# K transposed on VectorE instead of TensorE, scores against a block-diagonal q tile, and one row of w2 laid out on 64 partitions

## The chip, the core and the metric

The kernel is one program on one of the eight cores of a Trainium2 chip. The metric is the device time of one execution in microseconds, as the median of repeated runs; a lower one is better. A core has five engines, each with its own queue of instructions: TensorE (PE, matmuls, with its weight loads shown as PEld), VectorE (DVE), ScalarE (ACT), GpSimd (POOL) and SyncE (SP, which here only issues DMAs). Each engine works through its queue in order, and waits on semaphores for the others. The DMAs of all queues run on the core's 16 DMA engines.

## What is computed

One decode step of a transformer block, for a batch B of 2 with one new token each, D = 576, all in bf16. With xn the normalized x:

```
x + attention(xn) @ wo + relu(xn @ w1 + b1)^2 @ w2 + b2
attention: 32 query heads, 16 KV heads (2 queries share one), head size 128,
           the last 2048 positions of a cache of 8192
scores = q k^T / sqrt(128);  p = softmax(scores);  o = p v
```

Per batch entry and KV head, 2048 rows of K and of V are read once, 33.6 MB in all; wq, wo, w1 and w2 add 20.0 MB. So 53.6 MB have to come from memory for very little arithmetic.

## The kernel before

**Units.** The work on the cache is cut into 8 units (NU). A unit u is a group of TH = 4 KV heads of one batch entry: `tq, b = divmod(u, B)`. K of a unit is one tile of 128 partitions by 8192 bf16 (2 MB); a partition holds 64 consecutive positions of one head, and the four heads alternate over the partitions (partition 4c + h). V is laid out in the same way. K and V share one pool of 6 such buffers (`kvpool`, line 85), which go round in order of allocation, so each load waits until an earlier K or V has been used up.

**One unit's chain.** `transposes` (L258) turns K, taken as f32 pairs of bf16, by 128 by 128 transposes on PE against an identity, four to a PSUM tile of 1024 bf16; each tile is copied to SBUF by ACT (even groups, L270) or DVE (odd groups, L272). `scores` (L274) multiplies it by `qz`, a constant tile that holds the q of each unit among zeros: the stationary tile is 128 by 32, and four matmuls run side by side in four strips of 32 columns of the PE array. A first matmul with `far_h` writes -1e30 where query and key are of different heads. `softmax` (L288) takes the row maximum on DVE (L291), widens it (L293), takes the maximum over partitions with a GpSimd library call (`partition_all_reduce`, L295, tile `gmax`), forms the bias on DVE (L298), exponentiates on ACT (L302) and transposes p in 32 by 32 blocks on DVE (L305). `pv` (L314) multiplies by V, `pv_end` (L326) adds four partial results on DVE (L333, L335), and its `fin` (L338) sums over partitions on PE, divides, and writes the result to `ws` (L344 to L351).

**The order.** `step(u)` (L387) does the transposes and scores of unit u, `pv` of unit u-2 between them, and `softmax(u)`. All matmuls and transposes on PE keep the order of the source (the helpers `matmul` and `transpose`, L93 and L96, so nearly all PE work is shown at L94 and L97). The other engines' orders are chosen by the scheduler. After step 6, `mlp_h` (L356) computes the hidden layer from w1, which occupies the one `wbig` buffer; when its matmuls are done, `wo` is loaded into that buffer, followed on SP by w2 in pieces: `w2a` (rows of the first half), `w2b` (9 rows of each partition, in a K/V buffer) and `w2c` (6, 2 and 1 rows). Then come step 7, `pv_all(6)`, `pv_all(7)`, and `out_acc` (L216): four matmuls for each row of wo (32 rows) and w2 (36 rows), accumulated in `out_ps`; a copy by ACT and one DMA end the kernel.

**SP's queue**, in order: k0, wq, k1, v0, k2, v1, k3, v2, k4, v3, k5, v4, k6, v5, w1, k7, v6, v7, wo, w2a, w2b, w2c in three. In front of the loop, `q_block` (L226) computes q from wq, copies it with repetition to `qrow`, transposes it four times and copies it into `qz`.

Of the kernel before, what the change touches and what calls it, by code (L numbers as in the profile page):

```python
# [16 lines left out]
def kernel(  # L17
# [14 lines left out]
    nc = tc.nc  # L32
# [17 lines left out]
    JG = 8  # L50
    NG = NJ // JG
# [5 lines left out]
    TG = NG // NT  # L57
    QZ = 2 * NC
    assert SR == 32 and NG % NT == 0

# [15 lines left out]
    W2P = [(9, 15), (15, 17), (17, 18)]  # L76
    R9 = 9
# [15 lines left out]
    def matmul(*a, **k):  # L93
        tc.keep_in_program_order(nc.tensor.matmul(*a, **k))  # L94

# [20 lines left out]
    def issue_flat(w, name):  # L116
        n = w.shape[0] * w.shape[1] // P
        tl = wbig.tile([P, NH * L1], BF16, tag="wbig", name=name)
        nc.sync.dma_start(out=tl[:, 0:n], in_=w.rearrange("r n -> (r n)").rearrange("(p l) -> p l", p=P))
        return tl  # L120

    const.tile([P, 144], F32, name="pad_0")
# [15 lines left out]
    tmp_f = work.tile([P, 2, Dh], F32, tag="tmp", name="tmp_f")  # L138
# [50 lines left out]
    nc.vector.tensor_scalar(out=off[:], in0=own[:], scalar1=BIG, scalar2=-BIG, op0=ALU.mult, op1=ALU.add)  # L189
    of_h = const.tile([P, NC * WC], F32, name="of_h")  # L190
# [20 lines left out]
    w2c_sb = w2pool.tile([P, (FR - R9) * D], BF16, name="w2c")  # L211
# [8 lines left out]

    qz = const.tile([P, NQ, B, 2, 3 * QZ], BF16, name="qz")
    nc.gpsimd.memset(qz[:], 0.0)
# [3 lines left out]
    def q_block():  # L226
        for t in range(NH):
            for g in range(NG4):
                o = t * LQ + g * QW
                matmul(q_ps[32 * g:32 * g + 2 * B, :], lhsT=xnT[:, t].rearrange("p x b -> p (x b)"),  # L230
                       rhs=wq_sb[:, o:o + QW], start=(t == 0), stop=(t == NH - 1), skip_group_check=True,
                       tile_position=(0, 32 * g))
        row_t = const.tile([RB, 4 * HW], BF16, tag="row", name="qrow")
        qrow = row_t[:, 0:2 * QW]
        nh = QH // 2
        for k in range(2):
            cp = nc.scalar.copy if k else nc.vector.tensor_copy
            cp(out=qrow[:, k * QW:(k + 1) * QW].rearrange("p (i a d) -> p i a d", a=2, d=Dh),  # L238
               in_=q_ps[0:RB, k * QW // 2:(k + 1) * QW // 2].rearrange("p (i d) -> p i d", d=Dh).unsqueeze(2)
               .to_broadcast([RB, nh, 2, Dh]))  # L240
        qrow_f = qrow.bitcast(F32)
        qT_ps = psum.tile([P, QH * P], F32, tag="sc", bufs=2, name="qT_ps")
        for i in range(QH):
            transpose(out=qT_ps[:, i * P:i * P + RB], in_=qrow_f[:, i * Dh:(i + 1) * Dh],
                      identity=ident_f[0:RB, 0:RB])
        qT_v = qT_ps[:].bitcast(BF16).rearrange("p (i g e x b c) -> p b x g c e i", g=NG4 // 2, e=2, x=32 // B, b=B, c=2)
        hd = Dh // 2
        for j2 in range(2):
            cp = nc.scalar.copy if j2 else nc.vector.tensor_copy
            pp = slice(hd * j2, hd * (j2 + 1))  # L250
            o = QZ + NC * j2
            for b in range(B):
                for half in range(2):
                    cp(out=qz[pp, half * NQ // 2:(half + 1) * NQ // 2, b, :, o:o + NC].rearrange(  # L254
                        "p g c (e i) -> p g c e i", e=2), in_=qT_v[pp, b, half])

    kT_tiles, sc_tiles, pT_tiles, o1_tiles, o_tiles = {}, {}, {}, {}, {}
    def transposes(u, g):  # L258
        k_f = k_tiles[u][:].bitcast(F32)
        kT_ps = psum.tile([P, JG * P], BF16, tag="kT", bufs=3, name=f"kT_ps_{u}_{g}")  # L260
        kT_f = kT_ps[:].bitcast(F32)
        for i in range(JG // 2):
            j = g * JG // 2 + i
            transpose(out=kT_f[:, i * P:(i + 1) * P], in_=k_f[:, j * P:(j + 1) * P], identity=ident_f[:])
        t, o = divmod(g, TG)
        if o == 0:
            kT_tiles[(u, t)] = ktpool.tile([P, TG * JG * P], BF16, tag="kT_sb", name=f"kT_{u}_{t}")
        kT = kT_tiles[(u, t)][:, o * JG * P:(o + 1) * JG * P]
        if g % 2 == 0:
            nc.scalar.copy(out=kT, in_=kT_ps[:])  # L270
        else:
            nc.vector.tensor_copy(out=kT, in_=kT_ps[:])  # L272

    def scores(u, t):  # L274
        tq, b = divmod(u, B)
# [4 lines left out]
        kT = kT_tiles.pop((u, t))[:].rearrange("p (j k c) -> p j k c", k=P, c=2)  # L280
        z = QZ * (1 - t)
        for c in range(2):
            for g in range(4):
                matmul(sc_ps[32 * g:32 * (g + 1), :], lhsT=qz[:, tq, b, c, z:z + SR],
                       rhs=kT[:, :, 32 * g:32 * (g + 1), c], start=False, stop=(t == NT - 1 and c == 1),
                       skip_group_check=True, tile_position=(0, 32 * g))

    def softmax(u):  # L288
        sc_ps = sc_tiles.pop(u)
        m1 = work.tile([P, 1], F32, tag="m1", name=f"m1_{u}")  # L290
        nc.vector.tensor_reduce(out=m1[:], in_=sc_ps[:], axis=AX.X, op=ALU.max)  # L291
        m2 = work.tile([P, NC], F32, tag="m2", name=f"m2_{u}")
        nc.vector.tensor_scalar(out=m2[:], in0=off[:], scalar1=m1[:, 0:1], scalar2=None, op0=ALU.add)  # L293
        gmax = work.tile([P, NC], F32, tag="gmax", name=f"gmax_{u}")
        nc.gpsimd.partition_all_reduce(gmax[:], m2[:], channels=P, reduce_op=ReduceOp.max)  # L295
        gown = work.tile([P, NC], F32, tag="gown", name=f"gown_{u}")
        bias = work.tile([P, 1], F32, tag="bias", name=f"bias_{u}")
        nc.vector.scalar_tensor_tensor(out=gown[:], in0=gmax[:], scalar=-scale, in1=own[:], op0=ALU.mult,  # L298
                                       op1=ALU.mult, accum_out=bias[:])
        p_sb = work.tile([P, NJJ * 32], BF16, tag="p_sb", bufs=1, name=f"p_{u}")  # L300
        o1 = keep.tile([P, Dh + 1], F32, tag="o1", name=f"o1_{u}")
        nc.scalar.activation(out=p_sb[:], in_=sc_ps[:], func=ACT.Exp, bias=bias[:, 0:1], scale=scale,  # L302
                             accum_out=o1[:, Dh:Dh + 1])
        pT = keep.tile([P, NJJ, SR], BF16, tag="pT", name=f"pT_{u}")
        nc.vector.transpose(out=pT[:].rearrange("p j r -> p (j r)"), in_=p_sb[:])  # L305
        pT_tiles[u] = pT
        o1_tiles[u] = o1
# [4 lines left out]
    nc.gpsimd.memset(hT_sb[:], 0.0)  # L312

    def pv(u, part, parts):  # L314
        n = NJJ // parts
        if part == 0:
            o_tiles[u] = psum.tile([P, NS * Dh], F32, tag="o", name=f"o_ps_{u}")
        v = v_tiles[u][:].rearrange("p (t j s d) -> p j t s d", t=NT, s=2, d=Dh)
        for j in range(part * n, (part + 1) * n):
# [3 lines left out]
        if part == parts - 1:  # L323
            pT_tiles.pop(u)

    def pv_end(u):  # L326
# [3 lines left out]
        for k in range(NS):  # L330
            kw = dict(out=o1[:, 0:Dh], in0=o_ps[:, k * Dh:(k + 1) * Dh])
            if k == 0:
                nc.vector.tensor_scalar(scalar1=in_s[:, 0:1], scalar2=None, op0=ALU.mult, **kw)  # L333
            else:
                nc.vector.scalar_tensor_tensor(scalar=in_s[:, k:k + 1], in1=o1[:, 0:Dh], op0=ALU.mult, op1=ALU.add,  # L335
                                               **kw)

        def fin():  # L338
# [5 lines left out]
            nc.vector.reciprocal(out=linv[pp, :], in_=op[pp, Dh:Dh + 1])  # L344
            om_t = work.tile([P, Dh], F32, tag="om", name=f"om_{u}")
            om = om_t[pp, :].rearrange("p (q r) -> p q r", r=WR)
            nc.vector.scalar_tensor_tensor(out=om, in0=op[pp, 0:Dh].rearrange("p (q r) -> p q r", r=WR),
                                           scalar=linv[pp, 0:1], op0=ALU.mult, op1=ALU.mult,
                                           in1=own_c[pp, :].unsqueeze(2).to_broadcast([32, WC, WR]))
            with nc.allow_low_precision(reason="sums of one term and zeros"):  # L350
                nc.vector.tensor_reduce(out=ws[pp, :, BS * b], in_=om.rearrange("p q r -> p r q"), axis=AX.X,  # L351
                                        op=ALU.add)
# [3 lines left out]
    def mlp_h(w1_sb):  # L356
        h_ps = [psum.tile([P, HB], F32, tag="kT", bufs=3, name=f"h_ps_{k}") for k in range(2)]
# [28 lines left out]

    def step(u):  # L387
        fin = None
        w = u - 2
        with_pv = w >= 0  # L390
        for g in range(NG):
            transposes(u, g)
            if with_pv and g == 1:
                pv(w, 0, 2)
            if with_pv and g == 2:
                pv(w, 1, 2)
                fin = pv_end(w)
            if g == TG + 1:
                scores(u, 0)
            if g == TG + 2 and fin:  # L400
                fin()
        scores(u, 1)
        softmax(u)

    def pv_all(u):
        pv(u, 0, 1)
        pv_end(u)()

    for g in range(NG):
        transposes(0, g)  # L410
    q_block()
    for t in range(NT):
        scores(0, t)
    softmax(0)
    load_v(2)
    b1_rows = B_b1.rearrange("(x n) -> x n", n=HW)
    for i0, i1 in ((0, 2), (2, 4), (4, 6), (6, 8)):
# [3 lines left out]
    load_k(4)  # L421
# [16 lines left out]
    nc.sync.dma_start(out=w2a_sb[:], in_=w2_rows[0])  # L438
# [10 lines left out]
    for r in range(FR):  # L449
        w, o = (w2b_sb, r) if r < R9 else (w2c_sb, r - R9)  # L450
        out_acc(hT_sb[:, 1, r, :], w, o, stop=(r == FR - 1))
# [36 lines left out]
```

## Time and profile before

| | |
|---|---|
| median of 3 runs | 134.0 us (133.91 to 134.0) |
| the profiled execution | 133.92 us |
| its span, first to last instruction | 132.1 us |
| mean granted TensorE clock | 0.834 |
| busy: PE / PEld / DVE / ACT / POOL | 84.6 / 52.6 / 63.2 / 46.7 / 4.9 us |
| DMA moved, mean rate | 53.76 MB, 407 GB/s |
| DMA busy share of the SP queue's transfers | 95.2% of 16 engines' span |
| gmax of units 0 to 7 starts at | 28.29, 36.68, 45.63, 54.59, 63.78, 75.02, 83.97, 109.97 us |
| hidden layer's matmuls | 91.09 to 95.36 us |
| wo issued; first matmul with wo; last matmul | 95.41; 118.36; 129.24 us |

How to read it. The span is from the first to the last instruction of the one profiled execution, and all times within the kernel are counted from its start; the execution lasted 1.8 us longer than that. A busy time is the union of an engine's instructions, not what the kernel waits for. In a line of a group, "x8" is the number of instructions, then follow the busy time in us, the mean length of one in ns, and the idle time of the engine just ahead of them with what ended it. The chain that ended last is followed back from the end: each piece is what released the next.

### The profile page before, as it was taken

What the parts mean: (1) busy time and instruction counts of PE and PEld (TensorE: products, weight loads), DVE (VectorE), ACT (ScalarE), POOL (GpSimd) and SP (SyncE); (2) the same over time, 40 slices, a digit from 0 to 9 for tenths busy, and PEclk for the clock granted to TensorE, in tenths of its full rate; (3) what the DMA queues carried; (4) which work ended last, traced back from release to release, by engine and by line L of the source; (5) the groups of instructions that cost most, each with busy time, mean ns of one, the idle gap of its engine ahead of it and who ended that gap; (6) DMA issues with size and microseconds to landing.
All of it is one profiled execution on the core that took longest, in us unless ns stands there. A gap on an engine that the chain in (4) does not pass through costs nothing.

```text
span 132.1 us, 2285 instructions
## 1 busy us (share of the span) xinstructions
PE 84.6 (64%) x949; PEld 52.6 (40%) x949; DVE 63.2 (48%) x176; ACT 46.7 (35%) x67; POOL 4.9 (4%) x15
## 2 busy tenths in 40 slices
PE   0089319599589687697599787104819972739471
PEld 0069202286345353363455443002417640229360
DVE  7764400344557677396547687410075667550000
ACT  5725400339566085283256094200106632000000
POOL 5000000010010100100100100100000001000000
PEclk9999955959999999999779999855695999555955
DMA  4999899999999999999999999999999999899960
GB/s 160 397 437 526 369 388 442 422 432 432 429 432 422 442 417 427 437 432 437 432 427 414 437 488 402 445 424 405 427 427 442 468 435 458 376 408 418 418 255 1
DMA packets 3511, 53.76 MB, mean 407 GB/s; under 512 B 419, under 2 KB 558, under 8 KB 814
## 3 DMA queue, kind: packets, MB, share of 16 engines
q1 hardware_dynamic: 3456, 53.61, 95.2%
q8 instruction: 7, 0.11, 0.3%
q10 hardware_dynamic: 46, 0.02, 0.1%
q14 instruction: 2, 0.02, 0.0%
HBM read 53.62 MB, written 0.00 MB: 406 GB/s over the span
## 4 chain that ended last, share of the span: by engine, by line
DMA 78%; PE 15%; ACT 2%; SPq 1%; DVE 1%; issue 1%; ACTq 0%; DVEq 0%
DMA w<-in_B_w_dram 25%; DMA w2c<-in_B_w_dram 24%; DMA k<-in_A_k_cache_dram 16%; DMA wq<-in_A_wq_dram 13%; PE kT_ps L97 5%; PE h_ps L94 3%; PE q_ps L94 3%; PE sc_ps L94 2%; PE out_ps L94 1%; PE o_ps L94 1%; ACT kT L270 1%; DVE qrow L238 1%; SPq L106 0%; ACT qrow L238 0%; DVE qz L254 0%
## 5 line engine op out<-in xcount | busy, mean ns | idle before, releaser
L97 PE MATMUL kT_ps<-ident_f,k 128*128 128x128 f32 x256 | 41.4, 312 | 5.7 <-DMA k<-in_A_k_cache_dram 3.9
L97 PEld LDWEIGHTS kT_ps<-ident_f,k 128*128 128x128 f32 x256 | 32.9, 161 | 18.8 <-issue 9.9
L270 ACT COPY kT<-kT_ps 128x1024 bf16<-128x1024 bf16 x32 | 31.9, 1012 | 17.8 <-PE kT_ps L97 17.8
L272 DVE COPY kT<-kT_ps 128x1024 bf16<-128x1024 bf16 x32 | 21.8, 682 | 6.4 <-PE kT_ps L97 6.1
L94 PE MATMUL sc_ps<-kT,qz 128*32 128x512 bf16 x128 | 9.9, 388 | 6.7 <-DVE kT L272 4.7
L302 ACT ACTIVATE p<-sc_ps,bias 128x512 bf16<-128x512 f32 x8 | 5.5, 688 | 21.4 <-DVE gown L298 18.2
L94 PE MATMUL o_ps<-v,pT 128*32 128x512 bf16 x128 | 11.2, 429 | 0.0
L94 PEld LDWEIGHTS <-xnT 128*4 128x4 bf16 x108 | 3.5, 121 | 16.8 <-issue 15.2
L94 PE MATMUL h_ps<-w,xnT 128*4 128x288 bf16 x72 | 4.3, 429 | 8.0 <-DMA w<-in_B_w_dram 8.0
L305 DVE STREAM_TRANSPOSE pT<-p 128x512 bf16<-128x512 bf16 x8 | 5.7, 710 | 6.2 <-ACT p L302 6.2
L335 DVE SCALAR_TENSOR_TENSOR o<-o_ps,in_s,o 128x128 f32<-128x128 f32 x24 | 8.3, 345 | 0.4
L291 DVE TENSOR_REDUCE m<-sc_ps 128x1 f32<-128x512 f32 x8 | 5.5, 692 | 4.8 <-PE sc_ps L94 4.8
L375 DVE TENSOR_TENSOR hrow<-t 100x1152 bf16<-100x1152 f32 x2 | 2.6, 1355 | 9.6 <-ACT t L373 9.6
L94 PE MATMUL q_ps<-wq,xnT 128*4 128x512 bf16 x36 | 4.0, 627 | 4.9 <-DMA wq<-in_A_wq_dram 4.9
L295 POOL PARTITION_ALL_REDUCE gmax<-m x8 | 2.9, 367 | 104.9 <-DVE m L293 104.9
L94 PE MATMUL op_ps<-o,of_h 128*32 128x129 f32 x16 | 3.7, 316 | 4.6 <-DVE o L335 4.6
L456 ACT CAST fin_sb<-out_ps 113x144 bf16<-113x144 f32 x1 | 0.3, 280 | 17.9 <-PE out_ps L94 17.9
L94 PEld LDWEIGHTS <-qz 128*32 128x32 bf16 x128 | 2.1, 94 | 10.4 <-DVE kT L272 7.2
L97 PE MATMUL pro_ps<-ident,xn_sb 2*128 2x2 bf16 x5 | 0.9, 182 | 6.8 <-DVE xn_sb L171 6.5
L94 PEld LDWEIGHTS <-hT_sb 128*17 128x17 bf16 x144 | 3.4, 108 | 3.6 <-issue 3.5
L94 PE MATMUL out_ps<-wo,ws 128*17 128x144 bf16 x128 | 4.0, 325 | 1.2 <-DVE ws L351 1.2
L238 DVE CAST qrow<-q_ps 100x512 bf16<-100x512 f32 x1 | 0.7, 692 | 8.2 <-PE q_ps L94 8.2
(71 smaller groups left out, 57.4 us busy)
## 6 DMA issues: line engine op xcount, KB each, us to landing
k<-in_A_k_cache_dram SPq DMA_DIRECT2D x8, 2048.0 KB, 21.0
v<-in_A_v_cache_dram SPq DMA_DIRECT2D x8, 2048.0 KB, 21.5
w<-in_B_w_dram SPq DMA_DIRECT2D x1, 5184.0 KB
wq<-in_A_wq_dram SPq DMA_DIRECT2D x1, 4608.0 KB, 17.8
wo<-in_A_wo_dram SPq DMA_DIRECT2D x1, 4608.0 KB
w2a<-in_B_w_dram SPq DMA_DIRECT2D x1, 2592.0 KB, 26.9
w2b<-in_B_w_dram SPq DMA_DIRECT2D x1, 1296.0 KB
w2c<-in_B_w_dram SPq DMA_DIRECT2D x1, 864.0 KB
```

Source lines behind the costliest of these rows:

```text
L94: tc.keep_in_program_order(nc.tensor.matmul(*a, **k))
L97: tc.keep_in_program_order(nc.tensor.transpose(*a, **k))
L238: cp(out=qrow[:, k * QW:(k + 1) * QW].rearrange("p (i a d) -> p i a d", a=2, d=Dh), in_=q_ps[0:RB, k * QW // 2:(k + 1) * QW // 2].rearrang ...
L270: nc.scalar.copy(out=kT, in_=kT_ps[:])
L272: nc.vector.tensor_copy(out=kT, in_=kT_ps[:])
L291: nc.vector.tensor_reduce(out=m1[:], in_=sc_ps[:], axis=AX.X, op=ALU.max)
L295: nc.gpsimd.partition_all_reduce(gmax[:], m2[:], channels=P, reduce_op=ReduceOp.max)
L302: nc.scalar.activation(out=p_sb[:], in_=sc_ps[:], func=ACT.Exp, bias=bias[:, 0:1], scale=scale, accum_out=o1[:, Dh:Dh + 1])
L305: nc.vector.transpose(out=pT[:].rearrange("p j r -> p (j r)"), in_=p_sb[:])
L335: nc.vector.scalar_tensor_tensor(scalar=in_s[:, k:k + 1], in1=o1[:, 0:Dh], op0=ALU.mult, op1=ALU.add, **kw)
L375: nc.vector.tensor_tensor(out=h4[:, :, k * HB:(k + 1) * HB], in0=t4, in1=t4, op=ALU.mult)
L456: nc.scalar.copy(out=fin_sb[:], in_=out_ps[:])
```

## The change

K is transposed on DVE, two instructions for each unit, in blocks of 32 by 32 f32 pairs. The two copies out of PSUM and the PSUM tiles go. What this leaves in a column is spread over other partitions than with a full transpose, so `scores` now needs q placed block by block: the stationary tile is 128 by 128 and block-diagonal, and 16 matmuls of 512 columns use the whole array one after another. These tiles are made for each unit by a multiplication on GpSimd (`q_place`), alternately in two buffers, from the compact `qc`. DVE's instructions of a unit now keep the order of the source, and `step` has a new order. Row 17 of w2's second half goes to a tile `w2x` of 64 partitions with two rows each, by four DMAs behind w2a; `w2b` holds 11 rows and `w2c` 3, 2 and 1. b1 comes in 8 DMAs of one row instead of 4 of two; the load of k4 is issued before step 1.

```diff
-    qz = const.tile([P, NQ, B, 2, 3 * QZ], BF16, name="qz")
-    nc.gpsimd.memset(qz[:], 0.0)
+    qc = const.tile([P, NQ, B, NA, NC], BF16, name="qc")
+    qz = [const.tile([P, NA, P + QO], BF16, name=f"qz_{k}") for k in range(2)]
...
+    def q_place(u):
+        tq, b = divmod(u, B)
+        sh = [P, NA, NP4, NC]
+        nc.gpsimd.tensor_tensor(out=qz[u % 2][:, :, QO:].rearrange("p a (q c) -> p a q c", c=32)[:, :, :, 0:NC],
+                                in0=qc[:, tq, b].unsqueeze(2).to_broadcast(sh),
+                                in1=own_p[:].unsqueeze(1).unsqueeze(3).to_broadcast(sh), op=ALU.mult)
...
-    def transposes(u, g):
-        k_f = k_tiles[u][:].bitcast(F32)
-        kT_ps = psum.tile([P, JG * P], BF16, tag="kT", bufs=3, name=f"kT_ps_{u}_{g}")
-        for i in range(JG // 2):
...
-            transpose(out=kT_f[:, i * P:(i + 1) * P], in_=k_f[:, j * P:(j + 1) * P], identity=ident_f[:])
...
+    def transposes(u, t):
+        kT = ktpool.tile([P, UE // NT], BF16, tag="kT_sb", name=f"kT_{u}_{t}")
+        n = UE // NT // 2
+        tc.keep_in_program_order(nc.vector.transpose(out=kT[:].bitcast(F32),
+                                                     in_=k_tiles[u][:].bitcast(F32)[:, t * n:(t + 1) * n]))
+        kT_tiles[(u, t)] = kT
...
-        for c in range(2):
-            for g in range(4):
-                matmul(sc_ps[32 * g:32 * (g + 1), :], lhsT=qz[:, tq, b, c, z:z + SR],
-                       rhs=kT[:, :, 32 * g:32 * (g + 1), c], start=False, stop=(t == NT - 1 and c == 1),
-                       skip_group_check=True, tile_position=(0, 32 * g))
+        for i in range(NS // NT):
+            z = QO - NC * (t * NS // NT + i)
+            for h in range(2):
+                for e in range(2):
+                    matmul(sc_ps[:], lhsT=qz[u % 2][:, 2 * h + e, z:z + P], rhs=kT[:, i, :, h, :, e], start=False,
+                           stop=(t == NT - 1 and i == NS // NT - 1 and h == 1 and e == 1), skip_group_check=True)
...
     def step(u):
-        fin = None
         w = u - 2
-        with_pv = w >= 0
-        for g in range(NG):
-            transposes(u, g)
...
-        scores(u, 1)
-        softmax(u)
+        if w >= 0:
+            pv(w)
+        for t in range(NT):
+            scores(u, t)
+        fin = pv_end(w) if w >= 0 else None
+        rest = softmax(u)
+        if fin:
+            fin()
+        if u + 1 < NU:
+            q_place(u + 1)
+            transposes(u + 1, 0)
+        rest()
+        if u + 1 < NU:
+            transposes(u + 1, 1)
...
+    w2_last = w2_rows[1, :, RL * D:FR * D].rearrange("(e i q j) n -> e i j q n", e=2, i=2, q=4)
+    for i in range(2):
+        for e in range(2):
+            nc.sync.dma_start(out=w2x_sb[32 * i:32 * (i + 1), e, :], in_=w2_last[e, i])
```

`softmax` is cut in two: it issues the maxima and the all-reduce, and returns `rest`, which issues the bias, the exponential and the transpose of p. The hidden layer's values for `w2x` come from one more copy, transpose and two copies (`h_last`, `hx`, `hx_sb`).

In the built program, GpSimd's queue holds, ahead of each change between `q_place` and `gmax`, a pool configuration, the instruction pair that stands once in the program before. Its order is: configuration, q_place 0, 1 and 2, configuration, gmax 0, configuration, q_place 3, configuration, gmax 1, and so on to q_place 7, configuration, gmax 5, 6 and 7: 12 configurations for the one of before. q_place(u + 2) waits for the scores of unit u, whose tile it overwrites.

## The prediction, on record before the changed kernel was run

> **What bounds the kernel now.** I read the chain that ended last first, in order of time, then the groups by form, then GpSimd's own rows, then the timeline of a step.
>
> ```profile
> 33.63 20.86 DMA k<-in_A_k_cache_dram
> ...
> 58.00 33.05 DMA w<-in_B_w_dram
> 91.05 0.04 issue
> 91.09 4.30 PE h_ps L94 x71
> ...
> 96.74 31.12 DMA w2c<-in_B_w_dram
> 127.86 0.04 issue
> 127.90 1.36 PE out_ps L94 x36
> ```
>
> From 33.6 us on nearly all is a DMA in flight, and the queues' row on the page gives SP's transfers 95.2% of 16 engines' span. So the kernel streams 53.6 MB, and what the engines do is hidden as long as loads are issued in time. The steps before take 9.0 us (gmax starts at 36.68, 45.63, 54.59), against 9.75 us in which a unit's 4.2 MB arrive at 430 GB/s. Two places make compute count: wo can only be issued when the hidden layer's matmuls have ended (95.4; v7, ahead of it in the queue, runs out at 103.4, so there are 8 us to spare, less 1.4 us from an issue to its first packet), and the last work on units 6 and 7 must end before wo is due (wo's matmuls start at 118.4). A change that lengthens each of six steps by over 1 us uses this up.
>
> **The rows that price the change.**
>
> ```profile
> L272 DVE COPY kT<-kT_ps 128x1024 bf16<-128x1024 bf16 x32 | 21.8, 682 | 6.4 <-PE kT_ps L97 6.1
> L305 DVE STREAM_TRANSPOSE pT<-p 128x512 bf16<-128x512 bf16 x8 | 5.7, 710 | 6.2 <-ACT p L302 6.2
> L144 DVE STREAM_TRANSPOSE row<-tmp_f 128x32 f32<-128x32 f32 x1 | 0.2, 163 | 0.0
> ```
> ```profile
> L222 POOL MEMSET qz<- 128x768 bf16 x1 | 0.7, 739 | 0.3 <-POOLq L472 0.3
> ```
> ```profile
> L295 POOLq MODIFY_POOL_CONFIG  x2: 11/11/11, 2.5 to 2.6; - x2
> ```
> ```profile
> 28.29 0.37 POOL L295 PARTITION_ALL_REDUCE gmax<-m  x1 [25.79 <-DVE m L293]
> ```
>
> The reader is to see in them: (1) DVE transposes 512 bf16 in 710 ns and 32 f32 in 163 ns; (2) GpSimd writes 768 elements in 739 ns; (3) its pool configuration records 11 ns, but nothing used the configured library until 28.29.
>
> **Removed.** 256 transposes on PE (41.4 us busy), 32 copies on ACT (31.9) and 32 on DVE (21.8). All lie under the stream: worth nothing at the end by themselves.
>
> **K's transposes.** Two for each unit, 2048 f32 each. The two rows above give (710 - 163) / (512 - 32) = 1.14 ns per element and 0.13 us fixed: 2.46 us. Bounds: 1.4 us if they run at the copy's 0.67 ns per element, 4.8 us if a 4-byte element takes twice as long. I take 2.46, since one of the rows is f32 and shows no doubling. DVE's instructions keep the source order, so these stand in the chain of each step.
>
> **Scores.** 16 matmuls one after another instead of four strips side by side. In the trace, two that follow each other in one strip start 0.22 us apart (49.88 and 50.11, granted clock 1.0). At clock 0.5, q's 9 rounds of 512 columns took 4.04 us, 0.45 each. Eight of them wait for the second transpose: 1.9 us with the pipeline's tail, 3.7 at half clock. With long gaps on PE I take half clock (the rows of 84 to 95 us, when PE waited, have it).
>
> **q_place.** 512 elements on GpSimd. Bounds: 0.5 us at the memset's 0.96 ns, 1.5 with two reads beside the write. I take 1.0.
>
> **The pool configurations** decide. There were one, and are 12: six stand between q_place(u + 2), which itself waits until the scores of u are done, and gmax u. Queued behind each is gmax, for which DVE's bias waits, and behind that on DVE, in order, p's transpose, K's second transpose, and so the next scores. Below, the cost is nothing (11 ns); above, 25.7 us (2.56 to 28.29). A negative cost is excluded, as they are added in GpSimd's queue. Between: the packet records show wq's and K's packets at 38.5 to 39.6 ns per KB from 4 to 9 us, and 38.2 from 18 us on, as if something else read memory from 2.6 to about 9 us; ACT's table loads are over by 6. I take 6.4 us, though the slow packets may have another cause. Up to 3.0 us would be hidden: from the end of the scores, DVE needs 1.06 (maxima), 0.95 (`fin`) and 2.46 (first transpose of the next K), 4.5 in all, against 1.0 + 0.5 + configuration.
>
> The Trainium skill, "GPSIMD Engine Reference", section 2.1 Instruction dispatch, speaks against this change: the first call of a freshly loaded GpSimd kernel pays a load of its code of about 6 us, with no visible instruction. No row here shows that directly; by its 5.95 us instead of 6.4 the forecast would be 6 x 0.45 = 2.7 us lower.
>
> **The sum.** S_u is the end of unit u's scores, G_u that of its gmax. First unit: q_ps ends at 23.3; qrow's copies double in width (0.69 and 0.59 us for 512 columns: 1.2 and 1.0, one after the other), transposes and copies into qc 1.2, q_place 1.0, scores 5: S_0 = 32.9. G_0 = S_0 + 1.0 + 6.4 + 0.5 = 40.8. Then from G to the next G:
>
> ```profile
> 84.37 0.17 DVE L298 SCALAR_TENSOR_TENSOR gown<-gmax,own 128x8 f32<-128x8 f32 x1 [0.57 <-POOL gmax L295]
> 84.46 0.08 DVE L298 DVE_READ_ACCUMULATOR gown<-gmax,own 128x1 f32 x1
> 84.66 0.69 ACT L302 ACTIVATE p<-sc_ps,bias 128x512 bf16<-128x512 f32 x1 [3.15 <-DVE gown L298]
> 85.25 0.19 ACT L302 ACTIVATION_READ_ACCUMULATOR p<-sc_ps,bias 128x1 f32 x1
> 85.47 0.71 DVE L305 STREAM_TRANSPOSE pT<-p 128x512 bf16<-128x512 bf16 x1 [0.93 <-ACT p L302]
> ```
>
> This shows 1.84 us from gmax's end (84.34) to the end of p's transpose. Then K's second transpose 2.46, scores 3.7, q_place 1.0, configuration 6.4, gmax with its waits 0.5: **15.9 us a step**. (The configuration in front of q_place starts at G and ends 6.4 later, when the scores, at G + 8.0, are not done: hidden.) G_5 = 40.8 + 5 x 15.9 = 120.3, and S_6 = 128.3.
>
> From S_6 to the end PE leads: hidden layer 5.6 us (4.3 at the half clock of before, b1 and op); hrow's two products 3.0 as before, with p's and K's transposes between them on DVE 3.2; hidden transposes and copies 4.1 (98.4 to 102.5 before), for they hold the PSUM buffer that unit 7's scores need; these scores 4.5; from there to wo 9.6 before (108.8 to 118.4), plus 0.6 by the new order; 276 matmuls of out_acc 8.3 (before: 272 in 4.02 + 1.53 + 1.26 + 1.34); a wait of 1.1 like the 1.5 us at 123.8, which the profile calls issue and beside which lies an instruction packet of 16 KB. Sum 40.0: PE ends at 168.3 instead of 129.2, 39.1 later. wo, issued at about 134, has long landed. The end (0.3 copy, output) is as before. The profiled execution had 133.92: 133.92 + 39.1 = **173.0 us**; the median of the runs shown, 134.0, is 0.1 above it, which I leave out.
>
> **Edits hidden or small.** w2x: the records of the last row's packets (51 ns each, 8 on each DMA engine) end on eight engines at 126.7 to 127.3 us, on eight at 127.7 to 128.6, so one row less on the late ones is worth 0.4 us where the stream sets the end, and costs 0.4 if it goes to the late ones. The Trainium skill, "DMA: Bandwidth & Descriptors", section on why a DMA increments its semaphore by 16, says that a DMA uses as many engines as divide both outer sizes, here 8 of 32 and 8, the lowest; its rules for authors also say not to bother with partition halves. By the first rule this place is a gain of 0.4, by the second nothing; in my forecast the stream ends before PE and it is nothing either way. The two extra rounds of out_acc, hx's transpose and copies are 8 matmuls (0.3, counted) and four small copies beside other work. Eight DMAs for b1 instead of four, on ACT's queue, are done before ACT's first copy is due; four more issues of about 0.5 us on SP stand behind w2a, tens of us ahead of their data. k4's load moves ahead of step 1 past nothing but that step's issue-free work; its buffer comes free with K 1's second transpose (45 us), and SP waits there until then.
>
> **Rivals.**
>
> *A. The configurations cost under 3 us and DVE's chain is the bound.* Step: 1.06 + 0.95 + 2.46 + 1.15 (bias, exponential) + 0.75 + 2.46 + 1.9 = 10.7 us at full clock, 9.8 in the first two: S_6 = 95.4, PE ends some 39 later, at 134.4, 5.2 after 129.2: 139 us. For: nothing in the rows shows a configuration's cost. Against: the slow packets.
>
> *B. Faster.* If also a step takes at most 9.8 us (transposes of 2.0 us), S_6 comes by 90 and PE is done with wo's part in time; then the stream sets the end and w2x gives 0.4: 133.5 us. This decides at 9.8 us a step. For: 8 us to spare at wo, half the PE work gone. Against: the sum of rows is 0.9 above it.
>
> *C. f32 transposes at 4.8 us*, with the configurations: 2.35 more in each of six steps and in step 7: 173 + 16.5 = 190 us. Against: L144's 163 ns.
>
> That the change does not do what it says is excluded for PE and ACT: the built order has no K transpose there.
>
> **Chances.** Forecast 0.68, A 0.15, B 0.10, C 0.07. The forecast's own range: 4.5 us a configuration gives 161.6, 8.5 (then both of a step count) 188, full clock 11 less: 155 to 190. To leave out no more than 2 in 10 the range goes down to A: 136 to 190. A measurement of this kernel can tell about 0.2% (0.27 us) from no change. B's 0.10 is 0.07 faster, 0.02 the same, 0.01 slower; the rest is slower: 0.91.
>
> **What would show it.** Right: gmax starting 7 to 8 us after the scores end, 14 to 18 us apart in units 1 to 5, with DVE waiting for POOL; K's transposes at 2.4 to 2.5 us; DMA digits far under 9 after 55 us; wo issued near 134. Wrong: gmax within 2 us of q_place, steps of 10 to 11 us (A), or a chain that still ends in w2c's DMA (B).

## The result, and the profile after

The changed kernel takes **188.16 us** (median of 4 runs, 185.95 to 189.55) against 134.0 for the kernel before: a ratio of 1.391, with a 95% interval of 1.384 to 1.398. The profiled execution took 189.31 us (span 187.5, mean granted clock 0.727); two of the four runs, this one among them, lie over 1.5% above the fastest and are left out of the ratio.

The chain that ended last, which was one DMA after another before, now goes round through GpSimd. One step of it, from the maxima of unit 1 to the end of unit 2's scores (start, length, what):

```profile
52.66 0.70 DVE m L294
...
53.62 2.23 DVE kT L274
55.85 8.49 issue
64.33 0.40 POOL gmax L298
...
65.85 0.71 DVE pT L310
66.56 2.20 DVE kT L274
68.76 0.04 issue
68.80 3.58 PE sc_ps L96 x8
```

Of the 19.7 us from one end of the scores (52.64) to the next (72.38), 8.5 are "issue": GpSimd, whose next operation ends them, waits there for nothing that the profile shows. (PE works on the first half of unit 2's scores for 3.5 of these 8.5 us and loads run beside it, but the chain goes through neither.) Whom it holds up is told by the page's groups, whose last column is the idle time ahead of the group and what ended it:

```profile
L274 DVE STREAM_TRANSPOSE kT<-k 128x2048 f32<-128x2048 f32 x16 | 36.5, 2284 | 0.1
...
L303 DVE SCALAR_TENSOR_TENSOR gown<-gmax,own 128x8 f32<-128x8 f32 x8 | 1.3, 161 | 44.8 <-POOL gmax L298 44.8
...
L298 POOL PARTITION_ALL_REDUCE gmax<-m x8 | 3.1, 386 | 85.6 <-issue 57.1
...
L266 POOL TENSOR_TENSOR qz<-qc,own_p 128x128 bf16<-128x128 bf16 x8 | 3.1, 397 | 73.5 <-PE sc_ps L96 28.7
```

DVE waits 44.8 us for gmax, and GpSimd itself is idle for 57.1 us in front of six of its eight gmax with nothing to wait for, although it works for only 3.1 us on gmax and 3.1 on q. In that idle time lies only the pair of records of a pool configuration, and they are as short as in the kernel before (six pairs bear this line; the other six, in front of q_place, bear its line, with 4 to 108 ns):

```profile
L298 POOLq MODIFY_POOL_CONFIG  x12: 1/11/11, 34.2 to 132.0; - x12
```

So the price stands in no row of its own; it is read as the gap from the end of q_place to the start of gmax. The six gaps, as stretches of the timeline (length, POOL busy, granted clock, DMA share, GB/s):

```profile
core 0: us, POOL busy (x), PEclk, DMA share, GB/s
34.03:44.75 10.72, 0.01 (x2) 0.88 1.00 420
54.76:64.33 9.57, 0.00 (x1) 0.73 0.63 253
72.93:82.08 9.15, 0.00 (x1) 0.81 0.83 329
90.69:100.19 9.50, 0.01 (x2) 0.64 1.08 453
112.15:123.30 11.15, 0.00 (x1) 0.58 0.76 316
131.75:138.73 6.98, 0.01 (x1) 0.68 0.37 153
```

They are 9.5 us in the mean, and the shortest is the one in which the DMA engines did least. Otherwise their order is not that of the DMA share: the longest, 11.15 us, had 0.76. The loads have become the side work: their digits, nearly all 9 in the kernel before (first line), have holes in the changed kernel (second line) once the K and V buffers are held too long.

```profile
DMA  4999899999999999999999999999999999899960
```
```profile
DMA  6989999999599019913999989604700079899400
```

### The profile page after: what moved, and what is told of

It is laid out like the page before. It is cut to its first block, busy times and chain, and to the rows that moved or that the text cites. A ratio compares the mean times of both kernels' runs of the same rounds, so it can differ in the third digit from the quotient of the medians.

```text
span 187.5 us, 1780 instructions
## 1 busy us (share of the span) xinstructions
PE 85.5 (46%) x702; PEld 34.6 (18%) x702; DVE 80.0 (43%) x161; ACT 16.3 (9%) x38; POOL 8.8 (5%) x25
## 4 chain that ended last, share of the span: by engine, by line
DVE 29%; PE 28%; issue 25%; DMA 10%; ACT 4%; POOL 2%; SPq 0%; ACTq 0%; POOLq 0%
PE sc_ps L96 17%; DVE kT L274 15%; DMA wq<-in_A_wq_dram 10%; PE out_ps L96 4%; PE o_ps L96 3%; DVE pT L310 3%; ACT p L307 3%; DVE m L294 3%; PE q_ps L96 2%; DVE hrow L381 1%; POOL gmax L298 1%; DVE ws L357 1%; DVE o L341 1%; DVE om L353 1%; DVE m L296 1%
## 5 line engine op out<-in xcount | busy, mean ns | idle before, releaser
L96 PE MATMUL sc_ps<-kT,qz 128*128 128x512 bf16 x128 | 50.5, 567 | 64.8 <-DVE kT L274 64.5
L274 DVE STREAM_TRANSPOSE kT<-k 128x2048 f32<-128x2048 f32 x16 | 36.5, 2284 | 0.1
L96 PEld LDWEIGHTS <-qz 128*128 128x128 bf16 x128 | 16.3, 129 | 95.6 <-issue 92.2
L303 DVE SCALAR_TENSOR_TENSOR gown<-gmax,own 128x8 f32<-128x8 f32 x8 | 1.3, 161 | 44.8 <-POOL gmax L298 44.8
L96 PE MATMUL o_ps<-v,pT 128*32 128x512 bf16 x128 | 12.9, 481 | 0.0
L298 POOL PARTITION_ALL_REDUCE gmax<-m x8 | 3.1, 386 | 85.6 <-issue 57.1
L266 POOL TENSOR_TENSOR qz<-qc,own_p 128x128 bf16<-128x128 bf16 x8 | 3.1, 397 | 73.5 <-PE sc_ps L96 28.7
L96 PEld LDWEIGHTS <-xnT 128*4 128x4 bf16 x108 | 2.6, 95 | 15.1 <-issue 14.5
L96 PEld LDWEIGHTS <-pT 128*32 128x32 bf16 x128 | 4.6, 112 | 3.9 <-issue 2.4
L101 PE MATMUL hp<-ident,hrow 100*128 100x100 bf16 x18 | 1.7, 287 | 6.3 <-DVE hrow L381 6.3
L96 PEld LDWEIGHTS <-ws 128*17 128x17 bf16 x128 | 3.7, 136 | 1.5 <-DVE ws L357 1.5
L96 PE MATMUL sc_ps<-ident,far_h 4*128 4x512 bf16 x8 | 3.5, 439 | 0.0
```

The source lines that it names most:

```text
L101: tc.keep_in_program_order(nc.tensor.transpose(*a, **k))
L266: nc.gpsimd.tensor_tensor(out=qz[u % 2][:, :, QO:].rearrange("p a (q c) -> p a q c", c=32)[:, :, :, 0:NC], in0=qc[:, tq, b].unsqueeze(2).t ...
L274: tc.keep_in_program_order(nc.vector.transpose(out=kT[:].bitcast(F32), in_=k_tiles[u][:].bitcast(F32)[:, t * n:(t + 1) * n]))
```

## The experiments

My theory after this: the two kinds of GpSimd work, the multiplication of q_place and the all-reduce, exclude each other, each change between them costs some 10 us under the stream, and this alone is the loss. Rivals: the wait has another cause; the DVE chain and the full-array scores carry much of it.

**1. The change of kind by itself.** `mult` is a `tensor_tensor` of 128x128, `reduce` a `partition_all_reduce` of 128x8, both on GpSimd; during the second loop K and V are loaded.

```diff
+    for i in range(4):
+        mult()
+        reduce()
...
+    for i in range(5):
+        reduce()
+        mult()
```

> This kernel leaves out the whole block and writes zeros: GpSimd alternates between a multiplication of two 128x128 tiles and the all-reduce of a 128x8 tile, first with no load under way (9 changes, then three of each in a row), then while all of K and V stream (about 10 changes), then after the stream. Theory: each change of kind costs a library load that no record shows and that shares memory with the stream: 6 to 7 us from the end of one to the start of the next with no load (changed kernel, at 37% DMA share: 6.98), 9.5 to 11 us under the stream (at 100% share: 10.7), and nothing between two of a kind. Rival: what stood ahead of gmax was a wait on another engine, and the change of kind is cheap: under 1 us in all three stages. Second rival: a fixed price: the same 9 to 10 us in all stages.

Measured (stretches between two operations, columns as above; the first two lines lead to an all-reduce and to a multiplication with no load under way, the next four to a multiplication, an all-reduce, and again, under the stream, the last to a multiplication behind it):

```profile
18.90:24.80 5.90, 0.02 (x1) 1.00 0.00 0
25.20:31.80 6.60, 0.00 (x0) 1.00 0.00 0
...
83.40:95.10 11.70, 0.00 (x0) 1.00 1.00 422
95.60:106.40 10.80, 0.00 (x0) 1.00 1.00 422
106.90:118.90 12.00, 0.00 (x0) 1.00 1.02 426
119.40:129.20 9.80, 0.00 (x0) 1.00 1.01 426
...
151.30:158.10 6.80, 0.00 (x0) 1.00 0.00 0
```

With no load a change costs 5.9 to 6.1 us towards the all-reduce and 6.7 to 7.0 (once 7.7) towards the multiplication; with the DMA engines full, 9.9 to 10.9 and 11.6 to 12.2. Three of a kind in a row start without a gap (three all-reduces in 1.32 us). The first two changes, which were meant to be quiet, fell beside K's first loads and took 6.4 us (mean DMA share 0.75) and 10.2 us (0.47); so between no load and full engines the mean share of a gap does not give its length. Both rivals fall: the price is there with nothing to wait for, and it isn't fixed. The upper end under the stream is above the 11 us that I had given.

**2. The changed kernel without the changes of kind.** Two ways: q placed by ScalarE, and by GpSimd itself, but with copies (`nc.gpsimd.tensor_copy` in the same lines).

```diff
     def q_place(u):
-        nc.gpsimd.tensor_tensor(out=qz[u % 2][:, :, QO:].rearrange("p a (q c) -> p a q c", c=32)[:, :, :, 0:NC],
-                                in0=qc[:, tq, b].unsqueeze(2).to_broadcast(sh),
-                                in1=own_p[:].unsqueeze(1).unsqueeze(3).to_broadcast(sh), op=ALU.mult)
+        for q in range(NP4):
+            pp = slice(32 * q, 32 * (q + 1))
+            nc.scalar.copy(out=qz[u % 2][pp, :, QO + 32 * q:QO + 32 * q + NC], in_=qc[pp, tq, b])
```

> The changed kernel, but q goes to its diagonal places by four ScalarE copies of 32 partitions for each unit; GpSimd is left with the all-reduce and one configuration, all else as in the changed kernel. Theory (configurations hold the whole of each step up): the step falls from 18.8 us to m 0.95 + fin 0.95 + K's first transpose 2.27 + bias 0.2 + exponential 0.8 + p's transpose 0.71 + K's second 2.2 + half the scores 1.8 to 3.5 and gaps 0.1 = 10.0 to 11.7 us; scores of unit 6 end at 33.5 + 6 x 10.9 = 99 instead of 146.8, and with the same 37.9 us to the last matmul and 4.6 after it the time is 141 us (136 to 146). Rival (the DVE chain and the full-array scores at a low clock make up most of the 54 us): over 160 us.

> The changed kernel, with q placed by GpSimd itself and at the same places in its queue, but by four copies of 32 partitions instead of one multiplication; for copies the built program holds no configuration (one in all, as before). Theory (the change of library is the cost, not GpSimd's work in front of gmax): about 1 us of copies stands in front of gmax, beside the first transpose of the next K (2.27 us) and the rest of fin (0.95), so it is hidden: 136.4 us as with the copies on ScalarE (136 to 138). Rival (any GpSimd operation between scores and gmax costs the wait): over 180 us.

Measured: **136.43 us** with ScalarE (136.02 to 136.74; ratio to before 1.017, 1.015 to 1.019) and **137.06 us** with GpSimd's copies (136.36 to 137.34; 1.022, 1.020 to 1.024). 51 of the 54 us are gone. In GpSimd's timeline of the second, the copies start when the scores end, and gmax 0.20 us after the copies, held up only by the maxima:

```profile
43.34 0.94 POOL L267 COPY qz<-qc 32x32 bf16<-32x32 bf16 x4 [9.09 <-PE sc_ps L96]
44.48 0.37 POOL L297 PARTITION_ALL_REDUCE gmax<-m  x1 [0.20 <-DVE m L295]
```

So it is not work on GpSimd in front of gmax that costs the time, but the change of kind; the copies bring no configuration, and the built program holds one here as before. In this run it is recorded right in front of the first gmax, which starts 0.1 us behind it, with the DMA engines full:

```profile
L297 POOLq MODIFY_POOL_CONFIG  x2: 1/1/1, 33.8 to 33.8; - x2
```
```profile
33.90 0.36 POOL L297 PARTITION_ALL_REDUCE gmax<-m  x1
```

So a configuration as such costs nothing; what has the price is a change between the two kinds. (Experiment 1 has the same: its first multiplication, at 1.08 us, follows its configuration at 0.97.) Both kernels also end with that kind of operation, so its code may still have been in place from an execution before; no run tests that.

What remains of a step is DVE's chain with the second half of the scores, in the run with ScalarE:

```profile
71.00 1.91 PE sc_ps L96 x8
72.94 0.70 DVE m L293
...
74.90 2.31 DVE kT L273
77.39 0.79 ACT p L306 x2
78.20 0.71 DVE pT L309
78.91 2.21 DVE kT L273
81.16 1.91 PE sc_ps L96 x8
```

10.2 us here, 9.95 in the mean of six steps (scores of unit 0 end at 33.5, of unit 6 at 93.2): just over the 9.75 us of the stream. I had expected 141 us, since I put the end of unit 6's scores at 99, with steps of 10.9 us, the middle of 10.0 to 11.7 (half the scores at 1.8 to 3.5 us); in five of six steps half the scores took 1.9 us.

**3. The changes of kind alone, in the kernel before.**

```diff
         nc.gpsimd.partition_all_reduce(gmax[:], m2[:], channels=P, reduce_op=ReduceOp.max)
+        if u < 6:
+            dummy = work.tile([P, NC], F32, tag="dummy", name=f"dummy_{u}")
+            nc.gpsimd.tensor_tensor(out=dummy[:], in0=gmax[:], in1=gmax[:], op=ALU.mult)
```

> The kernel before, with one more GpSimd multiplication of 128x8 behind the all-reduce of units 0 to 5, whose output nobody reads: 13 configurations, and nothing else of the change. Theory: GpSimd needs two changes of kind of about 9.7 us for each unit, 20.2 us with the two operations, so gmax 6 starts at 28.3 + 6 x 20.2 = 149 instead of 84, and with the 41 us that the changed kernel needs from there the time is about 190 us (180 to 195). Rival (a configuration is cheap, the DVE chain costs the time): 134 to 136 us.

Measured: 184.84 us (182.03 to 188.63). Six multiplications of 0.2 us, whose output nobody uses, take the kernel before to nearly where the whole change took it:

```profile
28.51 0.37 POOL L295 PARTITION_ALL_REDUCE gmax<-m  x1 [26.01 <-DVE m L293]
39.87 0.20 POOL L298 TENSOR_TENSOR dummy<-gmax 128x8 f32<-128x8 f32 x1 [10.99 <-issue]
49.76 0.39 POOL L295 PARTITION_ALL_REDUCE gmax<-m  x1 [9.69 <-issue]
62.28 0.20 POOL L298 TENSOR_TENSOR dummy<-gmax 128x8 f32<-128x8 f32 x1 [12.13 <-issue]
```

Experiments 1 to 3 settle the cause: taken away, the loss goes; added alone, it comes; by itself, it has the size.

**4. Can the 2.4 us that remain be hidden?** DVE needs 8.85 us for a step, so I moved the next unit's first transpose and first half of scores ahead of the maxima.

```diff
     def step(u):
...
+        scores(u, 1)
         if u + 1 < NU:
             q_place(u + 1)
             transposes(u + 1, 0)
-        rest()
+            scores(u + 1, 0)
+        bias_exp, turn = softmax(u)
```

> The changed kernel with q placed by ScalarE, and a new order: the next unit's first K transpose and first half of scores stand ahead of the maxima, p v lies one unit deeper, and the hidden layer's transposes come after unit 7's scores. Theory: a step needs DVE for 2 x 2.27 + 0.95 + 1.5 + 0.2 + 0.95 + 0.71 = 8.85 us, under the 9.75 us in which a unit's data arrive, so the stream sets the end again: the last packets of w2c end at 128.4 us (copies on ScalarE: 128.43; before: 128.56), 133.8 us (133.4 to 134.2). Rival (the full-array scores at a granted clock near 0.5, 3.5 us a half, bind PE): a step of 10 us and 136 us.

Measured: 138.80 us (138.6 to 140.38; 1.038, 1.035 to 1.042): slower, against both expectations. From the maxima of one unit to those of the next it took 9.4, 7.6, 8.7, 10.2 and 10.3 us; in the last two half the scores took 3.5 and 3.4 us instead of 1.9, and DVE waited 1.4 and 1.3 us for them, as the rival had it. But at the end the order turned against itself (DVE's timeline, in brackets the idle time ahead and what ended it):

```profile
84.52 2.27 DVE L273 STREAM_TRANSPOSE kT<-k 128x2048 f32<-128x2048 f32 x1
96.77 2.31 DVE L273 STREAM_TRANSPOSE kT<-k 128x2048 f32<-128x2048 f32 x1 [9.98 <-DMA k<-in_A_k_cache_dram]
```

Unit 7's K comes behind w1, so its transpose waits 10 us, and the maxima of unit 6 and, on PE, the hidden layer stand behind it; wo was issued at 107.0 instead of 95.4. Mended by leaving unit 7 out of the look-ahead (`ahead` holds q_place, the first transpose and the first half of the scores), with w2x and with w2 as before:

```diff
+        if u + 1 < NU - 1:
+            ahead(u + 1)
...
+    pv_end(NU - 3)()
+    hrow = mlp_row(h_ps)
+    pv(NU - 2)
+    q_place(NU - 1)
+    transposes(NU - 1, 0)
```

> The last order mended where it lost: unit 7's K arrives behind w1 (its first transpose waited from 86.8 to 96.8 us there, and the maxima of unit 6, p v and the hidden layer's matmuls stood behind it), so unit 7's transposes and scores are no longer ahead of unit 6's; they follow the hidden layer's, p v of units 5 and 6 is drawn ahead of them. Theory: the steps at 8 to 10 us of the last run end unit 6's scores near 89 us, wo is issued by 98 us (in time is 102), unit 7 is done by 115, ahead of wo's landing at 118, and the stream sets the end: 134.2 us with w2x (133.9 to 134.6). Rival (what is left of the 2.4 us lies in the last unit's chain on DVE, whatever the order): 136 us or more.

> The same without w2x: w2's rows as in the kernel before (w2b 9 rows, w2c 6, 2 and 1), with K's buffers at a multiple of 512 bytes. Theory (w2x costs 0.4 us, as the aligned run of w2x alone measured, and the DVE transposes are hidden): 133.9 us (133.7 to 134.2), 0.2 to 0.5 below the run with w2x. Rival (w2x gains where the stream sets the end): 0.3 above it.

Measured: 135.07 us (134.37 to 135.75; 1.007, 1.005 to 1.010) and 135.32 us (134.11 to 135.98; 1.008, 1.005 to 1.011), both above what was expected, and the first below its rival's 136. The chain ends in DMAs again, in the run with w2x:

```profile
97.95 0.15 SPq L123
98.16 0.42 SPq L465
98.63 24.41 DMA w2x<-in_B_w_dram
123.06 6.79 DMA w2c<-in_B_w_dram
129.89 0.27 PE out_ps L96 x4
```

So DVE's transposes can be hidden but for about 1 us; no version beats the kernel before. What the last microsecond is remains open: w2c's last packet ends at 129.5 us here and at 129.0 in the run with the old w2, against 128.56 before, and single runs scatter over 1.9 us, more than the effect of w2x that the second run was to tell.

**5. w2x alone, and an address.**

```diff
-    W2P = [(9, 15), (15, 17), (17, 18)]
-    R9 = 9
+    R9 = 11
+    RL = FR - 1
+    W2P = [(R9, 14), (14, 16), (16, RL)]
...
+    for i in range(2):
+        for e in range(2):
+            nc.sync.dma_start(out=w2x_sb[32 * i:32 * (i + 1), e, :], in_=w2_last[e, i])
```

> The kernel before with only the last row of w2's second half on 64 partitions, two rows each, by four DMAs, and with w2b of 11 rows and w2c of 3, 2 and 1. Theory: the DMA engines that end late carry one packet of 51 ns for 8 partitions less: 133.6 us against 134.0 (133.4 to 133.8). Rival: the four small DMAs in front of w2b cost as much as they save, or the last packets go to the late engines: 134.0 to 134.4.

Measured: 135.34 us (135.0 to 135.57; 1.009, 1.008 to 1.011): 0.9% slower, and worse than the rival. In the packets' records nearly all were slower (those of 1,152 bytes alone kept 51 ns): 614 ns for 16,384 bytes instead of 611, from 20 us on, long before w2x. My edit had moved the K and V buffers to another start address. Three kernels part the two causes by a pad: w2x alone with 288 bytes more, the kernel before with 224 and with 256:

```diff
+    const.tile([P, 72], F32, name="pad_1")
...
+    const.tile([P, 56], F32, name="pad_1")
...
+    const.tile([P, 64], F32, name="pad_1")
```

> The run of w2x alone, with 288 bytes of padding, so that the K and V buffers start on a multiple of 512 bytes in a partition (31744) as in the kernel before (31232) and in the changed one (32768); without the padding they started at 31456. Theory: what w2x alone lost came from the address, since its K packets took 614 ns instead of 611 and its w2b packets 481 instead of 474 with copies on ScalarE; with the padding 133.8 us (133.5 to 134.1). Rival (the four small DMAs ahead of w2b, which put w2b's issue off by 5.2 us, cost it): 135.3 us again.

> The kernel before, with 224 bytes of unused padding behind the constants, so that all K, V and weight buffers start 224 bytes further on in a partition (31456 instead of 31232, no multiple of 512); nothing else is changed. Theory (the address slows the stream by about 0.5%): 135 us (134.7 to 135.4), K packets at 614 ns instead of 611. Rival (addresses don't matter): 134.0 us.

> The kernel before with 256 bytes of unused padding behind the constants: its buffers start at 31488, a multiple of 256 bytes and of 64, not of 512. Theory (only multiples of 512 run at the full rate): 134.85 us as with 224 bytes (134.6 to 135.1). Rival (multiples of 64 are enough): 134.0 us.

Measured: w2x on aligned buffers 134.39 us (134.24 to 135.32; 1.0035, 1.0019 to 1.0051); the kernel before with 224 bytes 134.85 us (134.72 to 135.1; 1.0067, 1.0055 to 1.0079), with 256 bytes 134.08 us (133.88 to 134.21; 0.9999, 0.9991 to 1.0008). The address is worth 0.8 us; a multiple of 256 is enough, and my "only multiples of 512" falls. w2x itself costs 0.37 us, where 0.2 gained was expected. Last, its four DMAs behind w2b instead of in front:

```diff
+    nc.sync.dma_start(out=w2b_sb[:], in_=w2_rows[1, :, 0:R9 * D])
     w2_last = w2_rows[1, :, RL * D:FR * D].rearrange("(e i q j) n -> e i j q n", e=2, i=2, q=4)
     for i in range(2):
         for e in range(2):
             nc.sync.dma_start(out=w2x_sb[32 * i:32 * (i + 1), e, :], in_=w2_last[e, i])
-    nc.sync.dma_start(out=w2b_sb[:], in_=w2_rows[1, :, 0:R9 * D])
```

> The aligned run of w2x alone, with its four DMAs issued behind w2b instead of in front of it, so that w2b is issued as early as in the kernel before. Theory (there is nothing to gain in w2x: 128 packets of 51 ns go and 128 come, and the packets of 1152 bytes add 9 ns a partition): 134.3 us again (134.2 to 134.5). Rival (w2b's later issue cost the 0.4 us, and the late engines do carry less): 133.6 to 133.9 us.

Measured: 134.43 us (134.27 to 135.51; 1.0032, 1.0010 to 1.0054). The place in SP's queue is not it.

## Why the prediction was right, and where it fell short

The mechanism, its place and the sign were right: six pool configurations between scores and gmax, with DVE, and by it PE and the loads, behind them. 173.0 us was 15 us too little, and the term that was mis-sized is the configuration.

- **The configuration behind q_place**, priced at 6.4 us: 10.7 in the first unit, 9.3 in the mean of the five steps. "As if something else read memory from 2.6 to about 9 us" gave a length, but those packets are no measure of a change of kind: in the run with GpSimd's copies, whose one configuration comes at 33.8 us, the packets from 4 to 6 us are as slow (41.8 and 40.5 ns per KB, and 37.9 to 38.5 from 6 to 9). Experiment 1 shows that 6.4 is within the price without load (5.9 to 7.0), to which the estimate came by luck, and that a full stream nearly doubles it. The same holds of the 6 us of the Trainium skill, "GPSIMD Engine Reference", section 2.1 Instruction dispatch: right where nothing else moves (5.9 to 6.1 us measured towards the all-reduce, 6.7 to 7.0 towards the multiplication), not under the stream (9.9 to 12.2); by it the forecast would have been 2.7 us further off.
- **The configuration in front of q_place**, costed at nothing because the scores cover it for 8.0 us: at 9 to 11 us the cover was too short twice. q_place of unit 3 started 1.73 us after the scores that release it (54.37 against 52.64), that of unit 6 3.52 us (111.76 against 108.24): 1.05 us a step. The forecast had named this case ("8.5, then both of a step count, 188") as the upper end of its own range. The kind of case came, but in two of five steps and with other terms smaller; that 188 is also the measured time is chance. So gmax came 7.5 to 15.1 us after the end of the scores, not 7 to 8, and 15.4 to 23.1 us apart, not 14 to 18.
- **The rest of the step.** q_place 0.40 instead of 1.0; K's transposes 2.28 (2.21 exposed) instead of 2.46, so no doubling for f32, and rival C falls; half the scores 3.4 to 3.6 instead of 3.7; gmax to the end of p's transpose 1.77 instead of 1.84. Per step: +2.9 and +1.05 for the two configurations, -0.6, -0.25, -0.2 and -0.1 for these: +2.8, and the end of gmax moved on by 18.8 us a step (45.14 to 139.13 in five) instead of 15.9.
- **The sum.** S_0 33.5 (32.9, though the terms as written add up to 32.7), G_0 45.1 (40.8), G_5 139.1 (120.3), S_6 146.8 (128.3), PE's end 184.7 (168.3). From S_6 on 37.9 us instead of 40.0: scores of unit 7 and what follows to wo took 17.0 instead of 14.7, but the hidden layer up to those scores 14.3 instead of 15.9 and out_acc 6.7 instead of 9.4, without the stall. wo was issued at 150.3, not near 134, and was never waited for, as foreseen.
- **Rivals A and B.** Experiment 2 is their condition, configurations at no cost: 136.4 us, between A's 139 and B's 133.5, with steps of 9.95 us between A's 10.7 and B's 9.8.
- **w2x** at 0.4 us gained where the stream sets the end: wrong in sign, 0.37 lost on aligned buffers. The step that failed is that one row less on the late engines would end the stream earlier. 128 packets of 1,152 bytes (51 ns) came, the packets of w2b and w2c lost as many bytes, and the last of these ended no earlier: at 128.73 us against 128.56. On which engines the new packets fell the records do not say. The Trainium skill's rule not to bother with partition halves ("DMA: Bandwidth & Descriptors", Rules for kernel authors), which I had set against it, was the better guide; its reason, that both halves spray over the same 16 engines, no run here tests. Where the 0.37 us come from is open: by the packets' lengths a partition takes 804 ns instead of 795, which with 8 partitions an engine is 0.07 us. In the changed kernel it hides, as the forecast had it.

## What to carry to other kernels

When an engine is given a second kind of library work, count how often it changes kind, and price each change by the gap in its timeline under the load of that stage, not by the record of the configuration. Two operations of a fraction of a microsecond that alternate can bind a kernel; with the same placement done by copies 2.4 us (ScalarE) and 3.1 us (GpSimd) of the 54 were left. A look-ahead in an in-order queue must stop where the data of the next unit is queued behind another load.

## What was not expected of the hardware

- A change of kind on GpSimd costs 5.9 to 7.0 us (once 7.7) with idle DMA engines and 9.9 to 12.2 us with full ones, more towards the multiplication than towards the all-reduce; with the engines partly busy it lay between 6.4 and 11.2 us, not in the order of the mean DMA share. A configuration with no other kind ahead of it in the kernel cost 0.1 us, under the stream too. What is fetched no record shows; that it shares memory with the stream is inferred from this.
- The start address of a buffer in a partition: 32 bytes past a multiple of 64 cost 3 ns on each packet (614 against 611 ns for 16,384 bytes, 1,536 against 1,533 for 41,472), 2 to 9 ns on the smaller ones at the end, and the kernel 0.8 us in all; a shift by 256 bytes left 611 ns. The 3 ns are the same for 16,384 and for 41,472 bytes, so they belong to the packet and not to its bytes. The Trainium skill, "DMA: Bandwidth & Descriptors", section on how a descriptor splits into AXI transactions, points the same way: a descriptor that does not start on a multiple of 256 bytes begins with a transaction of which a part is fetched and not used. The page says this of what is read; here the side that is written was shifted. Whether a multiple of 64 or 128 would do, no run here tells.
